# Attention scale turned once and spread through DRAM, part of the memory features moved from GpSimd to VectorE, and other matmul durations in the planner

## The chip, the cores and the metric

The kernel runs on one core of one Trainium2 chip. The metric is the device time of one execution in microseconds (us). The trace comes from one profiled execution of the same kernel. Engine names are those of the profile: PE is TensorE, DVE is VectorE, ACT is ScalarE, POOL is GpSimd, and SP is the sync engine, which issues nearly all transfers.

## The reference

Three stages follow each other: an attention with a recurrent memory, and two feed-forward blocks. B, H, S, D are 4, 8, 576, 64.

```python
def _attn_ref(q, k, v, M_prev, z_prev, beta):
    scores = np.where(causal, -1e9, scale * np.matmul(q, k.transpose(0, 1, 3, 2)))
    a = np.exp(scores - scores.max(-1, keepdims=True))
    a /= a.sum(-1, keepdims=True) + 1e-09
    local = np.matmul(a, v)
    def phi(x):
        return np.where(x > 0, x, np.exp(x) - 1.0) + 1.0
    q_p = phi(q)
    mem_ret = np.einsum('bhsd,bhde->bhse', q_p, M_prev)
    mem_norm = np.einsum('bhsd,bhd->bhs', q_p, z_prev)[..., None] + 1e-06
    g = 1.0 / (1.0 + np.exp(-beta))[None, :, None, None]
    return g * mem_ret / mem_norm + (1 - g) * local

x = attn_out.transpose(0, 2, 1, 3).reshape(B * S, H * D)   # 2304 x 512
h = x @ w_in                                               # 512 -> 2048
x = (np.maximum(h, 0) + np.log1p(np.exp(-np.abs(h)))) @ w_out
out = ((x @ w_a) * (x @ w_b)) @ w_out2                     # 512 -> 1536 -> 512
```

## The kernel before

**Attention in units.** A unit is one batch and one pair of heads; there are 16. The two heads lie on the upper and lower 64 partitions. For a unit the kernel computes five blocks of scores (`score(0)` to `score(4)`, matmuls of L494 and L510), takes each row's minimum on VectorE (L498, L511), the exponential and its row sum on ScalarE (L502, L515), turns the exponentials on TensorE (L558, L575, L576), copies them out with the gate applied (L564 on ScalarE, L566, L578 and L579 on VectorE), and multiplies by V (L588, L612). Everything after the scores of a unit runs one turn of the loop later, between the scores of the next unit.

**The memory path.** `prep_v` and `prep_v2` make the features phi(q) = exp(min(q, 0)) + max(q, 0): GpSimd takes the minimum (L476), ScalarE the exponential (L477) and the relu (L478), GpSimd the sum (L481). `memory` multiplies them by M and z (L525), and VectorE forms 1/(norm * rs) and the scaled product mo (L529 to L531). The product is turned (L600) and accumulated with the attention's in one PSUM bank.

**The scale.** rs is 1 / (sum of the exponentials), a column per row block and head (128 x 10). The finished product lies turned (features on partitions, rows along the free axis), so rs is needed as a row, repeated on 64 partitions. Before, `over` widens rs into R with GpSimd (L547), `spread` turns R with four transposes (L596), ScalarE copies the result out of PSUM (`rb`, L597), and `finish` does the same for the last 64 rows with two small matmuls (L620) and a copy (L624). VectorE then forms xx = product * rb (L608, L625), and xx is stored to `xs` in DRAM (L630).

**The feed-forward stages** use a fast matrix scheme (seven products for eight) with operands split in a high and a low part. `left_parts` decodes a weight block and splits it (rows of L708 to L712, L721, L321, L328), `right_parts` splits the activations (`x1h`, `x1l` and so on), `spill` decodes a block of the next weights and stores it. `BEFORE1` says ahead of which product unit of the first stage these are recorded (`w` a weight block, `x` an activation block, `s` a spill). The products are L826 (first and third stage) and L968.

**What sets the order.** No instruction is issued where the code stands. `Plan` records every step with what it reads and writes, `weigh` gives it a modelled duration, and `order` runs a list scheduler over engines; `emit` writes each engine's queue in the planned order. Attention is stream 0, the feed-forward stages are stream 1; on TensorE stream 0 goes first and inside a stream the code's order holds. On the other engines the step with the longest way to the end goes first. Steps that read and write SBUF only on VectorE or GpSimd carry `port`: the plan keeps VectorE's and GpSimd's apart in time, and a later GpSimd step waits for the VectorE step ahead of it. Each engine then works through its queue in order.

## Time and profile before

| | |
|---|---|
| median of 3 runs | 958.6 us (958.4 to 958.77) |
| profiled execution | 958.62 us, span 956.8 us |
| busy share: PE, DVE, ACT, POOL | 98%, 84%, 61%, 15% |
| TensorE clock granted | 1.00 of full speed over the whole span |
| attention, first product to last | 4.8 to 208.7 us |

The span is the stretch from the first to the last instruction; the execution's own time is 1.8 us longer. A busy PE is counted from records of pipelined matmuls, so the stage is read from the stretches and the waits as well. GpSimd works only in the attention.

### The profile page before, as it was taken

What the parts mean: (1) busy time and instruction counts of PE and PEld (TensorE: products, weight loads), DVE (VectorE), ACT (ScalarE), POOL (GpSimd) and SP (SyncE); (2) the same over time, 40 slices, a digit from 0 to 9 for tenths busy, and PEclk for the clock granted to TensorE, in tenths of its full rate; (3) what the DMA queues carried; (4) which work ended last, traced back from release to release, by engine and by line L of the source; (5) the groups of instructions that cost most, each with busy time, mean ns of one, the idle gap of its engine ahead of it and who ended that gap; (6) DMA issues with size and microseconds to landing.
All of it is one profiled execution on the core that took longest, in us unless ns stands there. A gap on an engine that the chain in (4) does not pass through costs nothing.

```text
span 956.8 us, 17107 instructions
## 1 busy us (share of the span) xinstructions
PE 938.2 (98%) x6316; PEld 898.7 (94%) x6316; DVE 803.7 (84%) x1491; ACT 579.8 (61%) x1156; POOL 139.4 (15%) x149
## 2 busy tenths in 40 slices
PE   6999999999999999999999999999999999999998
PEld 5887777789999999999999999999999999999998
DVE  4898788887999994998769999999999656899683
ACT  6988888876766666664445665444444334464443
POOL 8877767400000000000000000000000000000000
PEclk9999999999999999999999999999999999999999
DMA  7433444216699889746351243556554236762701
GB/s 239 118 111 112 135 131 119 76 59 229 210 318 317 308 297 369 310 150 222 116 198 50 93 140 136 179 199 237 190 184 154 97 114 209 264 204 85 231 34 50
DMA packets 82308, 167.33 MB, mean 175 GB/s; under 512 B 11568, under 2 KB 63536, under 8 KB 76976
## 3 DMA queue, kind: packets, MB, share of 16 engines
q1 hardware_dynamic: 81792, 165.91, 51.8%
q8 instruction: 49, 0.80, 0.3%
q10 hardware_dynamic: 432, 0.33, 0.1%
q14 instruction: 35, 0.29, 0.1%
HBM read 106.18 MB, written 60.03 MB: 174 GB/s over the span
## 4 chain that ended last, share of the span: by engine, by line
PE 90%; ACT 3%; POOL 3%; DVE 2%; DMA 1%; issue 1%; SPq 0%; DVEq 0%; POOLq 0%; ACTq 0%
PE bank L826 45%; PE bank L968 32%; PE bank L588 3%; PE bank L525 2%; PE bank L558 2%; POOL ph L476 2%; PE bank L494 2%; ACT eTrue L502 1%; PE bank L575 1%; ACT ph L477 1%; PE bank L612 1%; PE bank L596 1%; PE bank L600 1%; ACT aT L564 1%; PE bank L510 0%
## 5 line engine op out<-in xcount | busy, mean ns | idle before, releaser
L331 DVE TENSOR_TENSOR s<-bank,s 128x384 f32<-128x384 f32 x216 | 117.7, 554 | 35.5 <-PE bank L826 31.6
L804 ACT ACTIVATE s<-bank 128x384 f32<-128x384 f32 x72 | 34.9, 487 | 78.0 <-PE bank L826 45.3
L328 DVE TENSOR_TENSOR t<-t,t 128x1536 f32<-128x1536 f32 (+1 forms) x48 | 74.6, 1554 | 0.6
L826 PE MATMUL bank<-x1h,w 128*128 128x384 f32 x240 | 70.9, 336 | 1.5 <-ACT w L321 1.1
L826 PE MATMUL bank<-x7h,w 128*128 128x384 f32 x240 | 70.6, 334 | 0.9 <-ACT s L807 0.9
L826 PE MATMUL bank<-x5h,w 128*128 128x384 f32 x240 | 70.6, 334 | 0.0
L826 PE MATMUL bank<-x2h,w 128*128 128x384 f32 x240 | 70.5, 334 | 0.0
L826 PE MATMUL bank<-x3h,w 128*128 128x384 f32 x240 | 70.5, 334 | 0.0
L826 PE MATMUL bank<-x6h,w 128*128 128x384 f32 x240 | 70.5, 334 | 0.0
L826 PE MATMUL bank<-x4h,w 128*128 128x384 f32 x240 | 70.5, 334 | 0.0
L321 ACT ACTIVATE w<-wf 128x256 fp32r<-128x256 f32 (+1 forms) x100 | 50.0, 500 | 17.7 <-DVE w L328 11.1
L328 DVE TENSOR_TENSOR w<-wf,w 128x256 fp32r<-128x256 f32 (+1 forms) x100 | 53.3, 535 | 5.7 <-ACT w L321 5.5
L801 ACT ACTIVATE s<-bank 128x384 f32<-128x384 f32 x72 | 35.0, 487 | 35.3 <-PE bank L826 21.8
L862 ACT ACTIVATE s<-s 128x384 f32<-128x384 f32 x72 | 37.4, 522 | 27.3 <-DVE s L331 27.0
L321 ACT ACTIVATE gx2h<-t 128x768 fp32r<-128x768 f32 x37 | 31.3, 847 | 33.4 <-PE bank L968 30.9
L321 ACT ACTIVATE gx1h<-t 128x768 fp32r<-128x768 f32 x37 | 31.4, 847 | 33.2 <-PE bank L968 33.2
L321 ACT ACTIVATE gx0h<-t 128x768 fp32r<-128x768 f32 x37 | 31.4, 847 | 31.3 <-PE bank L968 28.1
L710 ACT ACTIVATE raw<-raw 128x512 f32<-128x512 f32 (+1 forms) x54 | 42.7, 802 | 10.6 <-DVE raw L709 9.7
L328 DVE TENSOR_TENSOR gx0l<-t,gx0h 128x768 fp32r<-128x768 f32 x37 | 35.4, 957 | 14.6 <-ACT gx0h L321 13.0
L807 ACT ACTIVATE s<-bank 128x384 f32<-128x384 f32 x72 | 35.3, 490 | 19.2 <-PE bank L826 14.6
L328 DVE TENSOR_TENSOR gx1l<-t,gx1h 128x768 fp32r<-128x768 f32 x37 | 35.4, 955 | 13.3 <-ACT gx1h L321 13.0
L321 ACT ACTIVATE gx3h<-t 128x768 fp32r<-128x768 f32 x36 | 30.5, 847 | 26.4 <-PE bank L968 26.4
(327 smaller groups left out, 3120.4 us busy)
## 6 DMA issues: line engine op xcount, KB each, us to landing
gs<-s SPq DMA_DIRECT2D x96, 192.0 KB, 4.5
t<-gs SPq DMA_DIRECT2D x24, 768.0 KB, 5.5
us<-s SPq DMA_DIRECT2D x72, 192.0 KB, 2.6
t<-us SPq DMA_DIRECT2D x12, 768.0 KB, 5.0
raw<-w_in SPq DMA_DIRECT2D x8, 1024.0 KB, 6.2
raw<-w_out SPq DMA_DIRECT2D x8, 1024.0 KB, 6.4
raw<-w_a SPq DMA_DIRECT2D x6, 1024.0 KB, 6.5
raw<-w_b SPq DMA_DIRECT2D x6, 1024.0 KB, 5.2
```

The costliest lines, as they stand in the source:

```text
L321: A.activation(out=o, in_=i, func=AF.Copy)
L328: eng.tensor_tensor(out=o, in0=a, in1=b, op=ALU.subtract)
L331: eng.tensor_tensor(out=o, in0=a, in1=b, op=ALU.add)
L476: G.tensor_scalar(out=self.ph, in0=self.qr, scalar1=0.0, scalar2=0.0, op0=ALU.min, op1=ALU.add)
L588: PE.matmul(out=self.po[both[j], 128 * k :], lhsT=self.vr[:, k, 64 * j : 64 * j + 64], rhs=a, start=False, stop=k == 3, skip_group_check=True,
L710: A.activation(out=f(high), in_=f(high), func=AF.Identity, scale=REBIAS)
L801: A.activation(out=self.s1, in_=bank["b"], func=AF.Copy)
L804: A.activation(out=self.s5, in_=bank["c"], func=AF.Copy)
L807: A.activation(out=self.s2, in_=bank["b"], func=AF.Copy)
L826: PE.matmul(out=o, lhsT=w(n, a, k), rhs=x[n][c][:, k], start=start and k == t == 0, stop=k == 1 and t == 2, skip_group_check=True,)
L862: A.activation(out=s, in_=s if bank is None else bank, func=AF.Softplus)
L968: PE.matmul(out=o, lhsT=self.w[n][a][:, u, 128 * m : 128 * m + 128], rhs=x[c][:, j], start=start and u == t == 0, stop=u == self.nu - 1 an ...
```

## The change

Four edits. First, in 14 of the 16 units (all but the first and the last, `near`) `send` turns rs once (128 x 10 to 10 x 128) right behind the memory products, copies it to SBUF on VectorE, writes it to DRAM (`rsd`, two transfers) and reads it back repeated on 64 partitions (two transfers, one for each head). R, its four transposes, the two small matmuls and both copies of ScalarE are kept for the two `near` units only. `rb` has two buffers. Second, ScalarE takes exp(q) without GpSimd's minimum, and one VectorE instruction forms min(exp(q), 1) + max(q, 0); both GpSimd steps go. Third, the plan takes other durations for plain fp32 products with 64 rows, and counts half a switch between transposes and products of one tiling. Fourth, `BEFORE1` records one spill ahead of product unit 18 in place of 7, and the ring of `s` buffers is listed in another order.

```diff
         if name not in self.state:
             return
+        if name in self.whole:
+            yield None, 1
+            return
...
-                s.mode = 128, 128
+                s.mode = 128, 128, True
...
-                s.time = max(2 * (n / 1.2 + 3) if plain else n / 2.4 + 13.3, cols * 0.42 * (128 // rows))
+                s.time = (1 + plain) * max(n / 1.2 + 3 if plain else n / 2.4 + 13.3, cols * 0.42 * (128 // rows))
...
-                        end += SWITCH
+                        end += SWITCH if not mode or s.mode[:2] != mode[:2] else SWITCH // 2
...
+    rsd = [kept([2, 5, 128], f"rsd{i}") for i in range(B * NP)]
+    plan.whole.update(t.tensor.name for t in rsd)
...
-            G.tensor_scalar(out=self.ph, in0=self.qr, scalar1=0.0, scalar2=0.0, op0=ALU.min, op1=ALU.add)
-            A.activation(out=self.ph, in_=self.ph, func=AF.Exp)
+            A.activation(out=self.ph, in_=self.qr, func=AF.Exp)
             A.activation(out=self.pos, in_=self.qr, func=AF.Relu)
 
         def prep_v2(self):
-            G.tensor_tensor(out=self.ph, in0=self.ph, in1=self.pos, op=ALU.add)
+            V.scalar_tensor_tensor(out=self.ph, in0=self.ph, scalar=1.0, in1=self.pos, op0=ALU.min, op1=ALU.add)
...
+            if not self.near:
+                self.send(banks[0:10, 0, 352:480])
...
+        def send(self, turned):
+
+            rt = take("rt")
+            PE.transpose(out=turned, in_=self.rs, identity=ident)
+            V.tensor_copy(out=rt[0:10], in_=turned)
+            d = rsd[self.b * NP + self.p]
+            SP.dma_start(out=d[:, 0:4].rearrange("j c q -> c j q"), in_=rt[0:8])
+            SP.dma_start(out=d[:, 4, 0:64], in_=rt[8:9])
+            for j, r in enumerate(both):
+                SP.dma_start(out=self.rb[r], in_=d[j].rearrange("c q -> (c q)")[0:S].partition_broadcast(64))
...
+            self.near = self.b * NP + self.p in (0, B * NP - 1)
+            if self.near:
+                self.R = blocks(take("R"))
...
-        0: "w0 w1 x0", 1: "x1", 3: "x2", 5: "w2", 7: "w3 s", 8: "s", 10: "w4 s", 11: "s", 13: "w5 s", 14: "s", 16: "w6 s", 17: "w7 s", 20: "t",
+        0: "w0 w1 x0", 1: "x1", 3: "x2", 5: "w2", 7: "w3", 8: "s", 10: "w4 s", 11: "s", 13: "w5 s", 14: "s", 16: "w6 s", 17: "w7 s",
+        18: "s", 20: "t",
```

On TensorE the order stays row for row, but for the removed and the added rows and six products of the first stage that move inside the last unit. On the other engines it moves throughout. Three places follow; line numbers of the changed kernel are shifted.

**VectorE, behind the memory products of the seventh unit.** nm is 1/(norm * rs), mo the scaled memory product, aT the turned exponentials, eTrue the row minima of the next scores, xx the finished product, rb the spread scale. Before:

```order
L529 SCALAR_TENSOR_TENSOR nm_124<-bank,rs_128 128x2x5
L530 RECIPROCAL nm_124<-nm_124 128x10
L531 TENSOR_TENSOR mo_100<-bank,nm_124 128x2x5x64
L566 TENSOR_SCALAR aT_112<-bank,og_60 128x512
L498 ISA eTrue_83,mn_123<-bank,mask_56 128x384
L498 ISA mn_123 128x1
L498 ISA eTrue_84,mn_123<-bank,mask_56 128x384
L498 ISA mn_123 128x1
L498 ISA eTrue_85,mn_123<-bank,mask_56 128x512
L498 ISA mn_123 128x1
L566 TENSOR_SCALAR aT_114<-bank,og_60 128x512
```

The same place in the changed kernel:

```order
L537 SCALAR_TENSOR_TENSOR nm_127<-bank,rs_131 128x2x5
L548 COPY rt_105<-bank 10x128
L538 RECIPROCAL nm_127<-nm_127 128x10
L539 TENSOR_TENSOR mo_100<-bank,nm_127 128x2x5x64
L589 TENSOR_SCALAR aT_114<-bank,og_60 128x512
L503 ISA eTrue_83,mn_126<-bank,mask_56 128x384
L503 ISA mn_126 128x1
L503 ISA eTrue_84,mn_126<-bank,mask_56 128x384
L503 ISA mn_126 128x1
L632 TENSOR_TENSOR xx_122<-bank,rb_120 128x512
L589 TENSOR_SCALAR aT_116<-bank,og_60 128x512
L650 TENSOR_TENSOR xx_122<-bank,rb_120 128x64
```

The copy of the turned scale stands between nm and its reciprocal, and the two xx rows here are those of the unit before; they stood at the end of their own unit.

**VectorE, the end of the same unit.** eT is the minimum of the fifth block of scores, a the tail's turned exponentials, w and wf are weight preparation, eFalse the first scores of the next unit. Before:

```order
L511 ISA eT_96,mn_123<-bank,mask_57 128x576
L511 ISA mn_123 128x1
L578 TENSOR_TENSOR aT_106<-bank,og_60 128x512
L579 TENSOR_TENSOR a_115<-bank,og_60 128x128
L328 TENSOR_TENSOR w<-wf,w 128x256
L721 TENSOR_TENSOR wf<-wf 128x256
L545 RECIPROCAL rs_129<-ss_127 128x10
L608 TENSOR_TENSOR xx_118<-bank,rb_117 128x512
L625 TENSOR_TENSOR xx_118<-bank,rb_117 128x64
L498 ISA eFalse_87,mn_122<-bank,mask_56 128x128
```

In the changed kernel:

```order
L601 TENSOR_TENSOR aT_108<-bank,og_60 128x512
L602 TENSOR_TENSOR a_117<-bank,og_60 128x128
L516 ISA eT_96,mn_125<-bank,mask_57 128x576
L516 ISA mn_125 128x1
L486 SCALAR_TENSOR_TENSOR ph_76<-ph_76,pos_78 128x640
L331 TENSOR_TENSOR w<-wf,w 128x256
L746 TENSOR_TENSOR wf<-wf 128x256
L503 ISA eFalse_87,mn_125<-bank,mask_56 128x128
```

The new sum of the features (ph) stands behind the last minimum of the unit. Further rows of weight preparation now stand between the next unit's minima and its nm, where before nothing stood.

**VectorE, the seventh weight block of the first feed-forward stage.** raw, wf and w are its decoding and its split, plain and more a spill, s the sums of the products. Before:

```order
L708 TENSOR_SCALAR raw_62<-raw_62 128x512 x2
L709 SCALAR_TENSOR_TENSOR raw_62<-raw_62 128x512 x2
L331 TENSOR_TENSOR s_141<-bank,s_141 128x384
L711 TENSOR_SCALAR raw_62<-raw_62 128x512 x2
L712 SCALAR_TENSOR_TENSOR wf<-raw_62 128x2x256 x2
L721 TENSOR_TENSOR wf<-wf 128x256
L331 TENSOR_TENSOR s_132<-bank,s_132 128x384
L721 TENSOR_TENSOR wf<-wf 128x256
L331 TENSOR_TENSOR s_131<-bank,s_131 128x384
L721 TENSOR_TENSOR wf<-wf 128x256 x2
L328 TENSOR_TENSOR w<-wf,w 128x256 x2
```

In the changed kernel:

```order
L736 TENSOR_SCALAR raw_63<-raw_63 128x512
L737 SCALAR_TENSOR_TENSOR wf<-raw_63 128x2x256 x2
L746 TENSOR_TENSOR wf<-wf 128x256
L737 SCALAR_TENSOR_TENSOR plain_146<-raw_62 128x1024
L334 TENSOR_TENSOR s_139<-bank,s_139 128x384
L746 TENSOR_TENSOR wf<-wf 128x256
L334 TENSOR_TENSOR s_138<-bank,s_138 128x384
L746 TENSOR_TENSOR wf<-wf 128x256 x2
L746 TENSOR_TENSOR more_149<-plain_147,more_149 128x256
L746 TENSOR_TENSOR more_148<-plain_146 128x256
L331 TENSOR_TENSOR w<-wf,w 128x256
```

Ahead of the last row of each piece stand, counted from the start of the stage, 48 sums of products and six decoded spills before, and 42 sums and five decoded spills in the changed kernel.

## Rows read from the trace of the kernel before

**Rows 1.** The page: an engine's busy time, then the chain that ended last.

```profile
PE 938.2 (98%) x6316; PEld 898.7 (94%) x6316; DVE 803.7 (84%) x1491; ACT 579.8 (61%) x1156; POOL 139.4 (15%) x149
...
PE 90%; ACT 3%; POOL 3%; DVE 2%; DMA 1%; issue 1%; SPq 0%; DVEq 0%; POOLq 0%; ACTq 0%
```

**Rows 2.** Stretches: length, busy us of each engine, granted clock, DMA share, GB/s.

```profile
30.70:89.00 58.30, 57.86 (x635) 47.20 (x636) 52.44 (x165) 51.57 (x142) 45.72 (x44) 1.00 0.41 119
89.00:188.10 99.10, 94.73 (x1016) 75.64 (x1016) 84.61 (x251) 86.16 (x236) 66.72 (x64) 1.00 0.39 117
...
255.00:350.00 95.00, 93.82 (x540) 93.18 (x539) 88.26 (x170) 64.58 (x129) 0.00 (x0) 1.00 0.89 303
```

**Rows 3.** Waits of PE over the span: us in total, times, longest.

```profile
PE bank L494 <- DVE kh L323: 5.1, 2, 4.8
PE bank L558 <- ACT aT L564: 3.6, 8, 0.8
PE bank L494 <- POOL kl L328: 1.5, 1, 1.5
PE bank L525 <- POOL mz L438: 1.2, 1, 1.2
PE bank L826 <- ACT w L321: 1.1, 1, 1.1
PE bank L826 <- ACT s L807: 0.9, 1, 0.9
```

**Rows 4.** The chain that ended last, from 138 us on: start, us, what.

```profile
140.19 2.36 POOL ph L476
...
142.57 0.74 ACT ph L477
...
144.43 0.57 ACT aT L564
```

**Rows 5.** PE's instructions in order of time, 48.7 to 53 us: start, us.

```profile
48.74 0.27 PE L576 MATMUL bank<-ident,eT 128*128 128x128 f32 x1
48.85 0.60 PE L596 MATMUL bank<-ident,R 128*128 128x128 f32 x4
49.29 0.60 PE L600 MATMUL bank<-ident,mo 128*128 128x128 f32 x4
...
52.61 0.29 PE L618 MATMUL bank<-ident,mo 128*64 128x64 f32 x4
52.72 0.29 PE L620 MATMUL bank<-ident,rs 128*64 128x64 f32 x4
52.94 0.33 PE L494 MATMUL bank<-kh,qh 64*128 64x128 f32 x2
```

**Rows 6.** Groups by form, 16.2 to 208.7 us: busy us, mean ns, idle before.

```profile
L476 POOL TENSOR_SCALAR ph<-qr 128x640 f32<-128x640 f32 x15 | 35.2, 2350 | 5.2 <-PE bank L525 5.2
...
L531 DVE TENSOR_TENSOR mo<-bank,nm 128x640 f32<-128x640 f32 x16 | 13.2, 825 | 0.5
...
L597 ACT ACTIVATE rb<-bank 128x512 f32<-128x512 f32 x16 | 9.4, 589 | 0.1
...
L579 DVE TENSOR_TENSOR a<-bank,og 128x128 f32<-128x128 f32 x16 | 4.5, 280 | 0.0
...
L712 DVE SCALAR_TENSOR_TENSOR wf<-raw 128x512 uint32<-128x512 uint32 x4 | 2.8, 694 | 0.1
```

**Rows 7.** DVE's and POOL's instructions in order of time, 94.2 to 98.3 us.

```profile
97.42 0.90 DVE L328 TENSOR_TENSOR w<-wf,w 128x256 fp32r<-128x256 f32 x1
...
96.62 1.42 POOL L328 TENSOR_TENSOR kl<-kr,kh 128x576 fp32r<-128x576 f32 x1
```

**Rows 8.** The group of the same DVE instruction, 209 to 360 us.

```profile
L328 DVE TENSOR_TENSOR w<-wf,w 128x256 fp32r<-128x256 f32 x18 | 7.6, 421 | 2.8 <-ACT w L321 2.7
```

**Rows 9.** Waits of DVE, 16.2 to 208.7 us.

```profile
DVE nm L529 <- PE bank L525: 12.6, 16, 2.9
```

**Rows 10.** DMA issues, 16 to 209 us: KB each, median us to landing.

```profile
vr<-vt SPq DMA_DIRECT2D x13, 32.0 KB, 2.7
```

More of the change, by code (lines that the diff above doesn't have):

```diff
@@ L61, in __init__ @@
         self.tc, self.steps, self.state, self.place, self.over = tc, [], {}, {}, {}
-        self.stream, self.exps, self.last = 0, [], {}
+        self.stream, self.exps, self.last, self.whole = 0, [], {}, set()
     def buffer(self, name, words, at, dtype=F32):
@@ L170, in weigh @@
                 rows, cols = (64 if x <= 64 else 128 for x in (kw["lhsT"].partition_size(), size(kw["lhsT"])))
-                s.time = max(2 * (n / 1.2 + 3) if plain else n / 2.4 + 13.3, cols * 0.42 * (128 // rows))
+                s.time = (1 + plain) * max(n / 1.2 + 3 if plain else n / 2.4 + 13.3, cols * 0.42 * (128 // rows))
                 s.time /= 16384 / rows / cols
-                s.mode = rows, cols
+                s.mode = rows, cols, False
         elif s.eng == "DVE":
@@ L390, in tile_kernel @@
     put("mz", NP * 65, spare(NP * 65), spare(NP * 65))
-    put("R", 512, late(512))
+    put("rt", 128, late(128), late(128))
+    put("R", 512, spare(512))
     put("aT", 512, *(late(512) for _ in range(10)))
     put("a4", 128, late(128), late(128))
-    put("rb", S, late(S))
+    put("rb", S, late(S), late(S))
     put("xx", S, late(S), late(S))
@@ L521, in memory @@
             nm = take("nm")
-            s = ps("psS", True)[:, :, 0:325].rearrange("p j (c e) -> p j c e", c=5)
+            banks = ps("psS", True)
+            s = banks[:, :, 0:325].rearrange("p j (c e) -> p j c e", c=5)
             for c in range(5):
@@ L545, in over @@
             V.reciprocal(out=rs, in_=self.ss)
-            self.R = R = blocks(take("R"))
-            G.tensor_scalar(
-                out=R.rearrange("p c (j e) -> p c j e", j=2), in0=heads(rs[:, 0:8], 4), scalar1=1.0, scalar2=0.0, op0=ALU.mult, op1=ALU.add,
-            )
+            self.rb = take("rb")
+            self.near = self.b * NP + self.p in (0, B * NP - 1)
+            if self.near:
+                self.R = blocks(take("R"))
+                G.tensor_scalar(
+                    out=self.R.rearrange("p c (j e) -> p c j e", j=2), in0=heads(rs[:, 0:8], 4), scalar1=1.0, scalar2=0.0,
+                    op0=ALU.mult, op1=ALU.add,
+                )
         def turn(self, eng, cols):
@@ L571, in turn_tail @@
             s = ps("psT")
-            self.a, self.a4, self.rb = a, a4, _ = take("aT"), take("a4"), take("rb")
+            self.a, self.a4 = a, a4 = take("aT"), take("a4")
             self.pt = pt = ps("t")
@@ L593, in spread @@
         def spread(self):
-            pr = ps("psS", True)[:, 0]
-            for c in range(4):
-                PE.transpose(out=pr[:, 128 * c : 128 * c + 128], in_=self.R[:, c], identity=ident)
-            A.activation(out=self.rb[:, 0:512], in_=pr, func=AF.Copy)
+            if self.near:
+                pr = ps("psS", True)[:, 0]
+                for c in range(4):
+                    PE.transpose(out=pr[:, 128 * c : 128 * c + 128], in_=self.R[:, c], identity=ident)
+                A.activation(out=self.rb[:, 0:512], in_=pr, func=AF.Copy)
             self.po = ps("o")
@@ L618, in finish @@
                 PE.matmul(out=pt[r, 0:64], lhsT=mo[:, 4, h], rhs=ident[:, h], start=False, stop=True, skip_group_check=True)
-            for j, r in enumerate(both):
-                PE.matmul(
-                    out=pt[r, 64:128], lhsT=self.rs[:, 8:9].to_broadcast([128, 64]), rhs=ident[:, 64 * j : 64 * j + 64],
-                    start=True, stop=True, skip_group_check=True,
-                )
-            A.activation(out=rb[:, 512:576], in_=pt[:, 64:128], func=AF.Copy)
+            if self.near:
+                for j, r in enumerate(both):
+                    PE.matmul(
+                        out=pt[r, 64:128], lhsT=self.rs[:, 8:9].to_broadcast([128, 64]), rhs=ident[:, 64 * j : 64 * j + 64],
+                        start=True, stop=True, skip_group_check=True,
+                    )
+                A.activation(out=rb[:, 512:576], in_=pt[:, 64:128], func=AF.Copy)
             V.tensor_tensor(out=xx[:, 512:576], in0=pt[:, 0:64], in1=rb[:, 512:576], op=ALU.mult)
@@ L877, in prepare1 @@
         if kind == "t":
-            put("s", HALF, *(47104 + HALF * i for i in range(6)), *(53760 + HALF * i for i in range(5)))
+            put("s", HALF, *(53760 + HALF * i for i in range(5)), *(47104 + HALF * i for i in range(6)))
             return
```

## The prediction

> **What bounds the kernel now.** I read the page first. TensorE is busy for 98% of the span, and the chain that ended last is 90% TensorE [rows 1]. So a change counts only where it takes work from TensorE's queue or a wait ahead of it. The waits of TensorE say which there are [rows 3]: one start-up wait for the first operands (4.8 us, which stays), eight waits of the transposes L558 for ScalarE's copy L564 (3.6 us), two waits for GpSimd at the start (1.5 and 1.2 us), and two in the first feed-forward stage (1.1 and 0.9 us).
>
> Then the stretches, cut at starts of the memory products L525 [rows 2]. From 30.7 to 89.0 us lie five units at 11.66 us each, in which TensorE misses only 0.44 us in all: this is TensorE's own pace. From 89.0 to 188.1 us lie eight units at 12.39 us each, 0.73 us slower, and TensorE's work is the same. Over all 13 units the period is 157.4 / 13 = 12.11 us. The chain says why the later ones are slow [rows 4]: GpSimd's minimum L476 (2.36 us) releases ScalarE's exponential, behind which the exponential of the scores and the copy L564 stand in ScalarE's queue, and L558 waits for that copy. The other number to keep is VectorE: 52.44 + 84.61 = 137.05 us busy in those 13 units, 10.54 us per unit. It idles 1.17 us per unit in the first five. The granted clock is 1.00 throughout (the 2.4 GHz level) and plays no part.
>
> **The change part by part.**
>
> *TensorE's own work, 14 units.* Four transposes L596 take 49.29 - 48.85 = 0.44 us. The two products L620 (four instructions) take 0.11 us: L618, of the same size, starts at 52.61 and L620 at 52.72; another 0.11 us up to L494 is the change of tiling, which stays [rows 5]. Removed: 0.55 us. Added is one transpose with a 128-column moving operand. The nearest row is the single transpose L576, 0.11 us. It stands between L525 and L558, where the tiling changes already, but its ten output rows are a shape that no row shows, so it costs between 0.11 and 0.33 us (two more changes at 0.11); I take 0.15 because it is a transpose of full depth like its neighbour. Net -0.40 us per unit, which makes TensorE's own pace 11.66 - 0.40 = 11.26 us.
>
> *The wait for GpSimd's minimum.* L476 goes, the exponential reads q directly and can run as soon as q has landed, a unit ahead; ScalarE also loses the copy L597 of 589 ns [rows 6] and the small copy L624. So the chain of [rows 4] is cut at its head, and if nothing took its place the eight slow units would fall to TensorE's pace as well.
>
> *What VectorE gets.* One scalar_tensor_tensor over 640 columns per unit. The nearest rows are the same operation over 512 columns, 694 ns, and a tensor_tensor over 640 columns out of PSUM, 825 ns [rows 6]; both overlap their neighbours by some 60 to 80 ns, so I take 0.75 us (bounds 0.69 and 0.87). The copy of rt from PSUM, 128 columns, has L579 as its nearest row, 280 ns with overlap; I take 0.20 us (0.15 to 0.28). VectorE's work per unit becomes 10.54 + 0.95 = 11.49 us, which is more than TensorE's 11.26. This is the term that decides: VectorE becomes the pace. What it idles now is mostly its wait at nm for L525: without the first unit's 2.9 us it is (12.6 - 2.9) / 15 = 0.65 us per unit [rows 9]. In the new order rows of weight preparation stand in that place, so the wait is filled with work. I leave 0.15 us per unit for what stays (an estimate; 0 if VectorE always has work, up to 0.65 if it still waits as before). The period is then 11.64, and I use 11.65 us. Over 13 units: 13 x (11.65 - 12.11) = -6.0 us. It holds only because the later part of the unit has room: behind the sum ph, TensorE still has L600, L588 and L612, so VectorE's delay there meets nobody for some microseconds; the five faster units gain almost nothing.
>
> *The scale's way through DRAM.* Four small transfers per unit on SP's queue. A 32 KB load takes 2.7 us from issue to landing [rows 10]; the write and the read back follow each other, 5.4 us, plus SP's issue of the loads of q, k and the store of the unit before that now stand among them. The consumer, xx, has moved a unit on: it stands behind the next unit's memory products and four minima. From the copy of rt to xx lies a whole period (11.65 us) and the seven rows between, some 14 us, against 6 to 9 us. So I cost it at nothing; cover is about 5 us. If it were late, VectorE would stand at xx, with the minima of the 512-wide scores behind it, which TensorE's next transposes need. rb's second buffer and the rt pair make reuse no issue: they come back two units later.
>
> *Start.* The first unit's two GpSimd steps (L476 alone 2.35 us [rows 6]) stand ahead of the second unit's kh, ql, kl and of mz. Without them TensorE's waits for kl (1.5) and mz (1.2) shrink [rows 3]; ScalarE's q for the second unit bounds the gain. I take -1.5 us (bounds -0.5 and -2.5).
>
> *Last units.* After 188.1 us there is one more unit without the transposes, -0.4 us.
>
> *First feed-forward stage.* TensorE's order is unchanged there. From 255 to 350 us VectorE is busy 88.26 of 95 us [rows 2], and TensorE waits once for a weight block, the seventh, 1.1 us by the list of waits and some 1.5 us with its second half [rows 3]. In the new order this block stands behind 42 sums and five spills where it stood behind 48 and six, so it comes earlier by more than the attention shrinks. I take the wait away, -1.5 us. The other wait (ScalarE, 0.9 us) is left as it is.
>
> *The planner's durations* have no cost of their own; they act by the orders above.
>
> Sum: -6.0 - 0.4 - 1.5 - 1.5 = -9.4 us on the profiled execution's 958.62 us, that is 949.2 us (its time equals the median of 958.6).
>
> **The rivals.**
>
> *TensorE stays the pace.* If VectorE's operations overlap well enough for 11.26 us per unit, the 13 units give 13 x (11.26 - 12.11) = -11.1, and the total is -14.5: 944.1 us. For it: in the first five units VectorE carried 10.49 us in 11.66 without holding TensorE. Against it: 11.49 us of work do not fit into 11.26.
>
> *VectorE keeps half or all of its old gaps.* With 0.65 us in place of 0.15 the period is 12.14, the units gain nothing, and what stays is start, end and weight wait: -3.0, 955.6 us. With part of it, 951 to 957.
>
> *VectorE's new sum stands behind GpSimd (slower).* At 97.42 us VectorE's subtraction of 256 columns took 0.90 us, where 18 of the same take 421 ns; GpSimd's kl ran until 98.04, and VectorE ended 0.28 us later [rows 7, 8]. So an SBUF-only VectorE operation that meets a GpSimd operation is held until that one ends. The new sum ph is of this kind, and kl (1.42 us) and ql run on GpSimd about when it comes up. If it is held for c us in each of 13 units and VectorE is the pace, the total is -9.4 + 13 c: no gain from c = 0.72, over 0.2% slower from 0.87, and 962 us at c = 1.0. For it: the plan keeps the two apart only in planned time. Against it: GpSimd loses L476's 2.35 us and two further steps of its 66.72 / 8 = 8.3 us per unit [rows 2, 6], so fewer meetings remain. The Trainium skill, page "SBUF — State Buffer", section "SBUF: two separate sides", states this as an exclusive lock between GpSimd and a VectorE operation with two SBUF inputs, held for the whole instruction; by that rule the trace agrees.
>
> *The scale comes late.* If the way through DRAM took over 14 us, VectorE would stand at xx in 14 units; 0.75 us late each eats the gain (about 959 us), and more makes it slower. Against it is the cover of 5 us.
>
> **How the numbers follow.** I give the forecast (946.5 to 952.5) 0.50, TensorE as the pace (942.5 to 946.5) 0.20, VectorE with its old gaps (952.5 to 958) 0.18, the held sum 0.08, the late scale 0.04. The range from 943.5 to 956 leaves out some of the second, the end of the third and the last two cases, about 2 in 10. A measurement here tells about 0.2%, 1.9 us. Faster than that is the forecast, TensorE's pace and most of the third case, 0.83; within it 0.08; slower 0.09, nearly all from the held sum and the late scale.
>
> **What would show it.** Right: the starts of L525 stand 11.5 to 11.8 us apart in every unit, VectorE is busy over 95% of the stretch, L558's waits for L564 are gone, and the last product of the attention ends some 8 us earlier. The weight wait near 341 us is gone. Wrong: L525 every 11.2 to 11.3 us (VectorE fits), or every 12 or more with a long ph on VectorE (held), a wait of VectorE at nm near 0.6 us (gaps stay), or one at xx for a transfer (late scale).

## The result and the profile after

The changed kernel takes 946.3 us (median of 4, 945.79 to 947.24) against 958.5 us (4 runs, 958.4 to 958.77). The ratio is 0.9873, with a 95% interval of 0.9856 to 0.989. It is 12.2 us faster, where 9.4 us were forecast.

First the page of the kernel after: busy time by engine, then the chain that ended last by engine. It answers to [rows 1].

```profile
PE 931.2 (99%) x6218; PEld 891.3 (94%) x6218; DVE 815.5 (86%) x1521; ACT 573.9 (61%) x1128; POOL 69.3 (7%) x103
...
PE 89%; DVE 10%; issue 1%; ACT 0%; DMA 0%; POOL 0%; DVEq 0%; ACTq 0%; POOLq 0%
```

TensorE lost 7.0 us of busy time, GpSimd half of its own, and GpSimd and ScalarE are gone from the chain (3% each before). VectorE is now in it with 10%, where it had 2%. That is some 94 us, about half of the attention's time, so by the chain alone VectorE is a candidate for the pace.

Next the waits of TensorE over the span (total, times, longest), which answer to [rows 3].

```profile
PE bank L499 <- DVE kh L326: 4.9, 1, 4.9
PE bank L499 <- POOL kl L331: 1.2, 1, 1.2
PE bank L531 <- POOL mz L444: 1.2, 1, 1.2
PE bank L531 <- DVE mn L503: 0.8, 3, 0.3
PE bank L581 <- ACT aT L587: 0.3, 1, 0.3
...
```

Of the eight waits of the transposes (now L581) for the copy aT one is left, and the two waits of the first feed-forward stage are gone from the list. The first three rows are the start.

Then the stretches: length, and the busy us of TensorE, its weight loads, VectorE, ScalarE and GpSimd. They answer to [rows 2]; the first is the 13 units, from the second memory product (L531) to the fifteenth, the second the seventh weight block's time.

```profile
29.10:177.30 148.20, 147.07 (x1563) 116.29 (x1561) 144.72 (x432) 130.26 (x349) 50.66 (x63) 1.00 0.49 141
...
250.00:345.00 95.00, 95.00 (x550) 95.00 (x549) 86.79 (x169) 63.52 (x128) 0.00 (x0) 1.00 0.91 301
```

The 13 units take 148.2 us, 11.40 us each, against 157.4 us (12.11 each). TensorE misses 1.13 us in all of them, and VectorE is busy 144.72 / 148.20 = 97.7%, 11.13 us per unit. In the second stretch TensorE misses nothing, where the kernel before missed 1.18 us.

Where the time came from, by the starts of the first memory product of each unit and the start of the last matmul (953.03 before, 940.19 after):

| part | forecast | measured |
|---|---|---|
| start of the first memory products (16.25 to 14.83), and the first interval (14.44 to 14.28) | -1.5 | -1.6 |
| 13 units (157.4 to 148.2) | -6.0 | -9.3 |
| the interval after them (10.70 to 10.42) | -0.4 | -0.3 |
| from the last memory products on (754.2 to 752.5), the weight wait in it | -1.5 | -1.7 |
| sum | -9.4 | -12.8 |

The two profiled executions are 12.8 us apart, the medians 12.2. So three of four terms were right within 0.2 us, and the 13 units gave 3.3 us more. In nine of the 13 the starts stand 11.24 to 11.42 us apart, in one 11.48; three are 11.54 to 11.57.

The next rows are from the kernel after in order of time (start, us): GpSimd's ql and VectorE's feature sum ph in one unit, then the sum of the next unit, where ql ran later.

```profile
94.21 1.56 POOL L331 TENSOR_TENSOR ql<-qr,qh 128x640 fp32r<-128x640 f32 x1
...
94.77 1.68 DVE L486 SCALAR_TENSOR_TENSOR ph<-ph,pos 128x640 f32<-128x640 f32 x1
...
106.11 0.82 DVE L486 SCALAR_TENSOR_TENSOR ph<-ph,pos 128x640 f32<-128x640 f32 x1
```

The sum takes 0.82 us alone, and 1.68 us when ql runs at its issue: ql ends at 95.77, and the sum 0.68 us later. In eight units it took 1.68 to 1.71. The Trainium skill (page "SBUF — State Buffer", section "SBUF: two separate sides") states an exclusive lock between GpSimd and a VectorE operation with two SBUF inputs; by that rule the trace agrees. The rival of the held sum did come about, at some 0.6 us per unit over the 0.75 that I took, and the units were still faster than forecast. That left one question open: is VectorE, 97.7% busy, the pace of the units at all?

### The profile page after: what moved, and what is told of

It reads as the page before. It is cut to its first block, busy times and chain, and to the rows that moved or that the text cites. A ratio compares the mean times of both kernels' runs of the same rounds, so it can differ in the third digit from the quotient of the medians.

```text
span 944.0 us, 16943 instructions
## 1 busy us (share of the span) xinstructions
PE 931.2 (99%) x6218; PEld 891.3 (94%) x6218; DVE 815.5 (86%) x1521; ACT 573.9 (61%) x1128; POOL 69.3 (7%) x103
## 4 chain that ended last, share of the span: by engine, by line
PE 89%; DVE 10%; issue 1%; ACT 0%; DMA 0%; POOL 0%; DVEq 0%; ACTq 0%; POOLq 0%
PE bank L851 46%; PE bank L994 32%; PE bank L499 2%; PE bank L611 2%; DVE eTrue L503 2%; PE bank L581 2%; PE bank L531 2%; DVE ph L486 1%; DVE aT L589 1%; DVE mo L539 1%; PE bank L515 1%; DVE eT L516 1%; DVE eFalse L503 1%; DVE aT L601 1%; PE bank L636 0%
## 5 line engine op out<-in xcount | busy, mean ns | idle before, releaser
L324 ACT ACTIVATE w<-wf 128x256 fp32r<-128x256 f32 (+1 forms) x100 | 49.8, 499 | 17.0 <-DVE w L331 12.2
L735 ACT ACTIVATE raw<-raw 128x512 f32<-128x512 f32 (+1 forms) x54 | 42.7, 802 | 12.3 <-DVE raw L734 11.8
L507 ACT ACTIVATE eTrue<-eTrue,mn 128x384 f32<-128x384 f32 (+1 forms) x64 | 42.2, 663 | 9.5 <-DVE mn L503 9.5
```

What stands on the lines that cost most here:

```text
L324: A.activation(out=o, in_=i, func=AF.Copy)
L507: A.activation(out=e, in_=e, func=AF.Exp, scale=-1.0, bias=mn[:, n : n + 1], accum_out=sm[:, n : n + 1])
L735: A.activation(out=f(high), in_=f(high), func=AF.Identity, scale=REBIAS)
```

## The experiments

Two theories stood against each other. **VectorE is the pace**: 11.13 us of work and what it waits make 11.40 us (my forecast's step, with the size off). **TensorE is the pace**: its own 11.25 us and small waits make 11.40, and VectorE is full because the planner puts weight preparation for the next stage into every hole. The kernels fall into two groups: parts of the change alone, and one cost added or taken away. This table has the results; the columns of us are read from the starts of memory products and the last matmul in each trace ("tail": from the last memory products to the last matmul). Each ratio is to runs of the kernel before that were taken along with it (medians of 958.5 to 958.7 us).

| kernel | median us | ratio to before (95%) | first product | each of 13 units | tail |
|---|---|---|---|---|---|
| before | 958.5 | 1 | 16.25 | 12.11 | 754.2 |
| after | 946.3 | 0.9873 (0.9856 to 0.989) | 14.83 | 11.40 | 752.5 |
| features alone | 958.6 | 0.9997 (0.9987 to 1.0006) | 14.78 | 11.67 | 760.8 |
| durations alone | 961.8 | 1.003 (1.0019 to 1.0041) | 16.35 | 12.40 | 752.7 |
| after without features | 961.2 | 1.0028 (1.0017 to 1.0039) | 16.40 | 12.00 | 758.1 |
| after, old durations | 948.1 | 0.9887 (0.9872 to 0.9902) | 15.70 | 11.42 | 754.2 |
| after, old spill order | 947.6 | 0.988 (0.9863 to 0.9896) | 14.70 | 11.40 | 753.3 |
| after, ql behind the sum | 953.0 | 0.9938 (0.9924 to 0.9953) | 15.33 | 11.38 | 759.0 |
| after, one more VectorE row | 954.7 | 0.996 (0.9945 to 0.9975) | 16.89 | 11.60 | 758.4 |
| after, two matmuls fewer | 949.1 | 0.9899 (0.9884 to 0.9914) | 14.83 | 11.25 | 758.0 |
| after, rt on ScalarE | 961.6 | 1.003 (1.002 to 1.004) | 15.50 | 12.05 | 757.5 |
| after, one hop more | 967.6 | 1.0085 (1.0067 to 1.0102) | 15.26 | 12.69 | 758.1 |
| after, two hops more | 997.8 | 1.0404 (1.0387 to 1.0422) | 14.75 | 14.74 | 758.0 |
| after, kh and kl first | 945.6 | 0.9861 (0.9846 to 0.9876) | 15.09 | 11.41 | 752.4 |

### Parts of the change

**Features alone.** The kernel before with this edit only:

```diff
-            G.tensor_scalar(out=self.ph, in0=self.qr, scalar1=0.0, scalar2=0.0, op0=ALU.min, op1=ALU.add)
-            A.activation(out=self.ph, in_=self.ph, func=AF.Exp)
+            A.activation(out=self.ph, in_=self.qr, func=AF.Exp)
...
-            G.tensor_tensor(out=self.ph, in0=self.ph, in1=self.pos, op=ALU.add)
+            V.scalar_tensor_tensor(out=self.ph, in0=self.ph, scalar=1.0, in1=self.pos, op0=ALU.min, op1=ALU.add)
```

> The kernel before with the feature edit alone (exponential straight from q, minimum and sum in one VectorE instruction), without the way through DRAM and with the planner's old durations. If the chain behind GpSimd's minimum is what made the eight later units slow, and TensorE's own pace of 11.66 us stays: 13 x (11.66 - 12.11) = -5.9, start -1.5, so about 951 us, and no wait of the transposes for the copy aT. If the held sum decides (0.5 us more in half the units) and the copies stay on ScalarE, the late units remain slow and only the start is gained: about 957 us. If the chain wasn't the cause at all: 957 us too, with the waits of the transposes still there.

The time is that of before, but the trace shows the expected gain and a loss that eats it. These are its 13 units (columns as above):

```profile
29.21:180.89 151.68, 151.31 (x1653) 123.39 (x1651) 139.00 (x416) 135.69 (x370) 58.54 (x78) 1.00 0.36 113
```

And from its list of TensorE's waits the longest:

```profile
PE bank L825 <- ACT w L321: 5.3, 1, 5.3
```

Twelve of the 13 units are 11.63 to 11.65 us, and TensorE misses 0.37 us in all. So GpSimd's two feature steps were the cause of the slow units (the edit takes both away at once; the chain of [rows 4] names the minimum), and the 11.66 us that I took for the pace without that chain was right. With the start that is -7.2 us up to the fifteenth memory products (188.13 to 180.89). In the first feed-forward stage a weight block comes 5.3 us late and the tail is 6.6 us longer. Part of this is the clock: behind that wait the granted clock is 0.50 in the stretch from 340 to 344 us, and TensorE's products run slower there. The planner had put less of the preparation beside the attention, where VectorE had the sum to do (on the tile raw, of which more below, 17.5 us in place of 22.0); that this made the block late is likely, but no run shows it by itself.

**Durations alone.** The kernel before with the planner's new durations:

```diff
-                s.time = max(2 * (n / 1.2 + 3) if plain else n / 2.4 + 13.3, cols * 0.42 * (128 // rows))
+                s.time = (1 + plain) * max(n / 1.2 + 3 if plain else n / 2.4 + 13.3, cols * 0.42 * (128 // rows))
...
-                        end += SWITCH
+                        end += SWITCH if not mode or s.mode[:2] != mode[:2] else SWITCH // 2
```

> The kernel before with the planner's new durations alone. No instruction is added or taken away, only places in the queues can move. If the durations have no weight of their own: 958.5 +- 1 us. If they are what takes the later units out of the chain behind GpSimd's minimum (rival): 13 units at 11.66 us, about 952 us.

It is 3 us slower, which neither expectation had. The units are 12.40 us and the waits for aT have grown, while the tail is 1.5 us shorter: the weight wait near 341 us is gone by this edit alone. From the list of TensorE's waits:

```profile
PE bank L558 <- ACT aT L564: 6.5, 12, 1.3
```

**After without the features.** The kernel after with minimum and sum back on GpSimd (the first diff turned round).

> The kernel after without the feature edit: minimum and sum of the features back on GpSimd, all else kept (way through DRAM, planner's durations, spill order). If TensorE's own pace is what counts everywhere: 14 units x -0.40, so about 953 us. If the chain behind GpSimd's minimum sets the later units whatever TensorE does: gain only in five units, about 956 us, with the transposes' waits for aT grown. If VectorE is the pace of the kernel after, this one, which has 0.8 us per unit less for it, is as fast as after in its units, and only the start (1.6 us) is lost: 948 us.

Its units are 12.00 us, 0.40 less than with the durations alone, as large as the term for TensorE's own work (-0.55 + 0.15). The chain behind GpSimd still sets these units, as its list of TensorE's waits shows in the first row; the second row is the largest piece of the tail's loss, the rows gx2 at the border of the two feed-forward stages.

```profile
PE bank L582 <- ACT aT L588: 5.9, 12, 1.2
...
PE bank L995 <- ACT gx2h L324: 2.6, 1, 2.6
```

That VectorE has less work here than in the kernel after and the units are 0.6 us longer speaks against its work as the pace, but not alone, since the chain explains it.

**After with the old durations.**

> The kernel after with the planner's old durations; no instruction added or taken away. My reading so far: alone, the new durations made the kernel before slower in its units (12.40 in place of 12.11 us) and took the weight wait near 341 us away. If they only act on that wait: units at 11.40 us as in after, the tail 1.5 us longer or, as in the run with the features alone, 8 us longer (a weight block 5 us late): 948 to 954 us. If the new durations are what lets the units run at TensorE's pace: units at 11.6 us or more, 950 to 957 us. If they do nothing here: 946.3 us.

The units are those of after (11.42): with GpSimd's chain gone the new durations no longer harm them. By the trace they give 0.8 us up to the last memory products and 1.7 us in the tail; the medians differ by 1.8 us, with intervals that overlap. The weight wait near 341 us is not back with the old durations either.

**After with the old spill order** and the old list of what is prepared when:

```diff
-            put("s", HALF, *(53760 + HALF * i for i in range(5)), *(47104 + HALF * i for i in range(6)))
+            put("s", HALF, *(47104 + HALF * i for i in range(6)), *(53760 + HALF * i for i in range(5)))
```

> The kernel after with the old order of the spill ring and the old list of what is prepared when in the first feed-forward stage. If the weight wait near 341 us went because of the new order of these: it is back, and the time is 1.5 us over after, 947.8 us. If it went because the attention's order left fewer sums ahead of the block (my step): same as after, 946.3 +- 0.5 us.

The intervals of this kernel and of after overlap, so the medians' difference of 1.3 us isn't shown. The trace has no weight wait near 341 us. The other gap, from one product's start to the next, which was 1.23 us near 382 us before and 0.44 after, is 1.23 us here, and the tail is 0.8 us longer. So the spill order and its list are worth that gap, and the weight wait went by the planner's order. The count of sums and spills that I gave as its reason isn't needed, since the durations alone removed it with the old lists.

### VectorE or TensorE

**ql behind the sum.** The kernel after, with GpSimd's ql made to wait until VectorE's sum has run, so that the two don't meet:

```diff
                 sub(e, self.ql[:, q], qr[:, q], f(self.qh[:, q]))
+                if e is G and plan.summed:
+                    plan.steps[-1].deps.add(plan.summed)
...
             V.scalar_tensor_tensor(out=self.ph, in0=self.ph, scalar=1.0, in1=self.pos, op0=ALU.min, op1=ALU.add)
+            plan.summed = len(plan.steps) - 1
...
-            if nxt and n:
-                nxt.prep_k()
             if cur:
                 cur.prep_v2()
+            if nxt and n:
+                nxt.prep_k()
```

> The kernel after with GpSimd's ql put behind VectorE's feature sum, so that the two no longer meet (in half the units of after the sum was held by ql, 1.70 us in place of 0.82). If VectorE is the pace: it gets back 0.86 us in half the units, the units fall to TensorE's own 11.25 us, 13 x -0.15 = -1.9, so 944.4 us. If TensorE is the pace: 946.3 +- 0.5 us with VectorE's sum at 0.82 us in all units. If ql, now later, holds other VectorE instructions in its turn: no change, with the longer means elsewhere.

The group of the sum in the 13 units (busy us, mean ns), first of the kernel after, then of this one:

```profile
L486 DVE SCALAR_TENSOR_TENSOR ph<-ph,pos 128x640 f32<-128x640 f32 x13 | 17.7, 1364 | 0.0
```

```profile
L488 DVE SCALAR_TENSOR_TENSOR ph<-ph,pos 128x640 f32<-128x640 f32 x13 | 10.7, 826 | 0.0
```

This kernel's 13 units as a stretch, and then VectorE's longest wait in them:

```profile
29.54:177.50 147.96, 147.20 (x1560) 116.27 (x1560) 141.30 (x434) 129.52 (x350) 51.86 (x64) 1.00 0.48 143
```

```profile
DVE nm L540 <- PE bank L550: 4.4, 6, 0.9
```

The hold is gone: 0.83 us in place of 1.36, 7.0 us in 13 units. The period stays: 11.38 us in place of 11.40. VectorE took part of the time for more weight preparation and waited for TensorE (nm) with the rest; it is 95.5% busy. It has also left most of the chain that ended last, as the page of this kernel shows:

```profile
PE 92%; DVE 4%; issue 0%; DMA 0%; ACT 0%
```

So the held sum had no price, because VectorE's total was not the pace, though in the kernel after half of the attention's chain ran through it. The whole kernel is slower by its tail (+6.5 us), where gx2 comes late as in the kernel without features, and by 0.5 us at the start.

**One more VectorE row.** The kernel after with one instruction more per unit:

```diff
+            V.scalar_tensor_tensor(out=self.ph, in0=self.ph, scalar=1.0, in1=self.ph, op0=ALU.min, op1=ALU.min)
             V.scalar_tensor_tensor(out=self.ph, in0=self.ph, scalar=1.0, in1=self.pos, op0=ALU.min, op1=ALU.add)
```

> The kernel after with one more VectorE instruction of 640 columns per unit, which changes no value (minimum of the feature sum's input with itself and 1, which the sum takes anyway). If VectorE is the pace: its 0.82 us, or 1.3 us with holds by GpSimd, are added to 11.13 us per unit, and the period becomes 12.0 to 12.4: 13 x 0.6 to 1.0 = +8 to +13 us, about 956 us. If TensorE is the pace and VectorE has only work that can lie elsewhere (weight preparation that the planner fills in): the preparation is pushed out of the units and the time stays at 946 to 948 us.

The two groups in its 13 units:

```profile
L486 DVE SCALAR_TENSOR_TENSOR ph<-ph 128x640 f32<-128x640 f32 x13 | 19.3, 1483 | 0.0
L487 DVE SCALAR_TENSOR_TENSOR ph<-ph,pos 128x640 f32<-128x640 f32 x13 | 10.7, 826 | 1.0
```

The 13 units as a stretch, and then TensorE's longest wait in them:

```profile
31.24:182.05 150.81, 147.02 (x1563) 116.29 (x1561) 147.62 (x426) 125.11 (x339) 56.99 (x65) 1.00 0.45 134
```

```profile
PE bank L532 <- DVE mn L504: 2.9, 9, 0.4
```

The two take 30.0 us where after had 17.7, 0.95 us more per unit (the hold by ql now falls on the first). The period grew by 0.20. The rest came out of the preparation. These are the instructions on the tile raw alone in the 13 units, first of after, then of this kernel; behind the length stands VectorE's busy us, then ScalarE's.

```profile
29.10:177.30 148.20, 19.32 (x31) 10.28 (x19) 1.00 0.49 141
```

```profile
31.24:182.05 150.81, 13.88 (x23) 7.82 (x15) 1.00 0.45 134
```

By the groups of VectorE that write raw, wf, w and the rows x, preparation in the 13 units sums to 30.6 us before, 25.2 after and 15.3 here. Outside the units the kernel loses 2.1 us up to the first memory products and 5.9 us in the tail. Of these, 4.4 us come early in the first feed-forward stage with a weight block that is 1.9 us late, behind which the granted clock is 0.50 from 246 to 248 us. That the block is late because its preparation was put off is likely, but no run shows it by itself. My second expectation had the right mechanism and no price for the tail.

**Two matmuls fewer.** The kernel after without the kh and ql products of the fifth score block (that block loses precision):

```diff
-                for t, (a, b) in enumerate(terms):
-                    PE.matmul(out=s[:, c, :288], lhsT=a[:, 512:640], rhs=b[:, cs], start=t == 0, stop=t == 2)
+                for t, (a, b) in enumerate(terms[:2]):
+                    PE.matmul(out=s[:, c, :288], lhsT=a[:, 512:640], rhs=b[:, cs], start=t == 0, stop=t == 1)
```

> The kernel after without the product of kh with ql in the fifth block of scores: two matmuls of 288 columns per unit (0.13 us each) are left out, so that block's scores have less precision; TensorE's other rows stay in their order, and VectorE has as much work as before. If TensorE is the pace in the units of after: 0.26 us less per unit, 11.14 us, 13 x -0.26 = -3.4 and a little at both ends, 942.5 us. If VectorE is the pace: 11.40 us per unit as in after, 946 us. Since VectorE was busy 11.13 us per unit, a mixture (11.2 to 11.3 us) would say that both are near their limit.

Its 13 units:

```profile
28.92:175.19 146.27, 145.49 (x1537) 112.54 (x1535) 142.21 (x434) 130.33 (x349) 49.53 (x64) 1.00 0.46 143
```

The period fell by 0.15 us to 11.25, and six units are at 11.13 to 11.14. TensorE's removed work is 0.26 us. From the start of that block to the last transposes behind it (L515 to L599) the time falls by 0.10 us only, so 0.16 us per unit is lost again to waits right there. VectorE is busy 10.94 us per unit, no longer 11.13, with the same instructions of the unit's own: the sum met ql for a shorter time (15.4 us in the 13 units in place of 17.7). This run alone could therefore be read for VectorE as well; the run with ql behind the sum, which took three times as much from the sum and left the period, speaks against it. Taken together, the units follow TensorE by more than half when its work is cut, and don't follow VectorE when its time is cut. The kernel as a whole is 2.8 us slower than after, by a tail that is 5.5 us longer with gx2 late.

**rt on ScalarE.** The kernel after with the copy of the turned scale moved:

```diff
-            V.tensor_copy(out=rt[0:10], in_=turned)
+            A.activation(out=rt[0:10], in_=turned, func=AF.Copy)
```

> The kernel after with the copy of the turned scale moved from VectorE (0.27 us per unit) to ScalarE. If VectorE is the pace of the kernel after (my step, 11.40 us per unit with VectorE 97.6% busy), its units get shorter, at most to TensorE's own pace of 11.25: up to 13 x -0.15 = -1.9, so 944.4 us. If TensorE is the pace and what lies over 11.25 are waits of another origin: 946.3 +- 0.5 us. If ScalarE's copies aT come late by it: up to +2 us, with the transposes' wait for aT back.

It is slower by 15 us, which no expectation had. From its list of TensorE's waits:

```profile
PE bank L499 <- DVE mo L539: 6.4, 9, 1.0
```

And from one unit VectorE and TensorE in order of time (start, us):

```profile
68.30 0.75 DVE L589 TENSOR_SCALAR aT<-bank,og 128x512 f32<-128x512 f32 x1
68.96 0.81 DVE L539 TENSOR_TENSOR mo<-bank,nm 128x640 f32<-128x640 f32 x1
...
69.92 0.50 PE L499 MATMUL bank<-kh,qh 64*128 64x512 f32 x2 [0.95 <-DVE mo L539]
```

In the new plan VectorE takes aT ahead of mo in such units. mo empties the PSUM banks of the memory products, into which the 512-wide scores go next, and TensorE stands 0.95 us. In the 13 units such waits are 5.5 of the 8.5 us that these lose against after; another 5.0 us are the tail, again with gx2 late. VectorE has less to do than in the kernel after; one place in its order costs more than the work saved.

### The scale's way through DRAM, and the start

One and two further copies from DRAM to DRAM on the way, in the kernel after:

```diff
+            for far in hops:
+                o = far[self.b * NP + self.p]
+                SP.dma_start(out=o.rearrange("j c q -> j (c q)")[:, 0:S], in_=d.rearrange("j c q -> j (c q)")[:, 0:S])
+                d = o
```

> The kernel after with two more copies from DRAM to DRAM on the scale's way (each another write and read of the same few KB, by SP's queue), nothing else changed. My step costs this way at nothing under a cover of about 5 us. In the trace of after the read is issued about 5 us before the product xx, and lands some 2.5 us before it. Two hops add about 5 us: if the cover is as forecast, VectorE stands at xx for some 0 to 0.5 us per unit, 946 to 953 us. If the cover is only the 2.5 us, each unit is 2 to 3 us longer, 970 to 985 us. If the planner moves xx a unit further, nothing: 946.3 us.

> The kernel after with one further copy from DRAM to DRAM on the scale's way (two were 3.3 us more per unit). One hop is a transfer of about 2.7 us and its issue on the queue. With a cover of 5 us, as forecast: 946.3 +- 1 us. With the 2.5 us that the trace of after shows between the landing of the scale and the product xx: 0.5 to 1 us more per unit, 953 to 960 us. If it isn't the latency but the further rows on the queue that delay the loads of q, k and v: half of the two hops' price, 1.7 us per unit, 968 us.

One hop costs 1.29 us per unit, two 3.34. Not all of it is waiting: for the same instructions TensorE is busy 153.67 us in the 13 units with one hop and 162.57 with two, where it is 147.07 in after, and the mean granted clock of these stretches is 0.98 and 0.93, where it is 1.00. From the lists of TensorE's waits, one hop, then two:

```profile
PE bank L604 <- DVE xx L655: 10.2, 7, 1.8
```

```profile
PE bank L604 <- DVE xx L655: 30.4, 12, 4.4
```

It isn't VectorE that stands at xx for the scale, as I had it (0.3 us in all with two hops, none with one). xx comes later in VectorE's order, and TensorE stands at the last transpose of the block's tail (L604 here, L599 in after), whose bank xx has to empty. In after xx ends at 115.54 us and that transpose starts at 115.59. So the scale's way is hidden as it is, but there is no room to put xx later. Since the planner moved xx by its own durations for the copies, the runs don't show how late the scale itself would have been, nor what part the queue's further rows have in the price.

**kh and kl first.** The kernel after with the second unit's ql on GpSimd put behind its kl:

> The kernel after with GpSimd's order at the start turned: the second unit's kh and kl ahead of its ql (in after TensorE waits 0.3 us for kh, 1.2 for kl and 1.2 for mz there). If these waits are what is left of the start chain and TensorE is the pace of all that follows: the first memory products stand 0.8 to 1.3 us earlier and the whole kernel gains as much, 945.2 us. If the chain through mz and the held feature sum sets the start in any case: 946.3 us. If the changed row count moves the later plan to the worse order at the boundary of the feed-forward stages: 951 to 953 us with the units unchanged.

No gain: the waits moved. GpSimd's and VectorE's kl in order of time (start, us), and TensorE's wait:

```profile
5.94 1.56 POOL L331 TENSOR_TENSOR kl<-kr,kh 128x576 fp32r<-128x576 f32 x1
...
6.16 2.03 DVE L331 TENSOR_TENSOR kl<-kr,kh 128x256 fp32r<-128x256 f32 x2
```

```profile
PE bank L502 <- DVE kl L331: 2.0, 1, 2.0
```

The first unit's kl on VectorE (0.42 and 0.49 us in after) is held by GpSimd's kl until 7.50 us. TensorE loses at the first unit what it gains at the second. Its 945.6 us can't be told from after, and no kernel here is clearly better than after.

## Why the prediction was right, and where its size was off

**Direction and range** were right: 946.3 us lies in 943.5 to 956. But it lies just outside the forecast's own part of it (946.5 to 952.5) and just inside that of the rival in which TensorE stays the pace (942.5 to 946.5), and the period of 11.40 us lies between the sign of being right (11.5 to 11.8) and that of being wrong (11.2 to 11.3). The step that was to decide the time failed, so the number was met in part by luck.

**The start, the last unit and the weight wait** came out within 0.2 us. The start is the feature edit's (14.78 with it alone, 16.40 without it). The weight wait did go, but my reason for it isn't needed: the planner's durations alone remove it. The agreement of the whole tail (-1.7 us for -1.5) is partly chance: the weight wait gave -1.6 us, the gap near 382 us, which I had left as it is, gave -0.9, and the last unit's end lost 0.8.

**TensorE's own work.** The shortest units are 11.63 us with the features alone and 11.24 in after, -0.39 where -0.40 was forecast; two errors cancel in this. The transposed scale is a row of its own in the order of time of the kernel after:

```profile
40.68 1.54 PE L531 MATMUL bank<-mz,ph 64*128 64x65 f32 x20
42.15 0.28 PE L547 MATMUL bank<-ident,rs 128*10 128x128 f32 x1
42.26 0.38 PE L581 MATMUL bank<-ident,eFalse 128*128 128x128 f32 x2
```

From its start to that of L581 it takes 0.11 us, the low bound of my range, and the transposes behind it take 0.05 us less than they did, so the work fell by 0.50 us. The other 0.10 us are a wait that the lists of waits do not show. Here are VectorE and TensorE in one unit of the kernel after, then TensorE in one of the kernel before (start, us):

```profile
99.25 0.27 DVE L548 COPY rt<-bank 10x128 f32<-10x128 f32 x1
...
99.68 0.82 DVE L539 TENSOR_TENSOR mo<-bank,nm 128x640 f32<-128x640 f32 x1
...
100.56 0.49 PE L499 MATMUL bank<-kh,qh 64*128 64x512 f32 x2
100.89 0.40 PE L499 MATMUL bank<-kl,qh 64*128 64x512 f32 x2
```

```profile
57.00 0.39 PE L494 MATMUL bank<-kh,qh 64*128 64x512 f32 x2
57.23 0.40 PE L494 MATMUL bank<-kl,qh 64*128 64x512 f32 x2
```

In all 13 units of after the first 512-wide scores start 0.05 to 0.06 us behind the end of mo and the next ones 0.33 us behind them; before, the starts stood 0.26 us behind mo and 0.23 apart. With the copy rt ahead of its reciprocal, mo starts 2.29 to 2.47 us behind the memory products, where it was 2.03 with the features alone. The twelve score products L499 between the transposes take 1.55 us on average, where they took 1.42 with the features alone. So TensorE stands some 0.1 us at mo in every unit, and its own pace lies nearer to 11.15 than to the 11.24 of the shortest units (forecast 11.26). That the copy rt is the reason is read from the order of time; the run that moved it to ScalarE changed the order in other ways too.

**The step that failed** is "VectorE's work per unit becomes 10.54 + 0.95 = 11.49 us, which is more than TensorE's 11.26. This is the term that decides: VectorE becomes the pace." Both added prices were too low (the sum 1.36 us with its holds, the copy 0.27), and the step was wrong all the same: the 10.54 us held some 2.35 us of preparation for the next stage (30.6 us / 13), which isn't due in its unit. After the change 25.2 us of it stand there, 0.41 us less per unit, and the tail did not pay for it. What remains between 11.24 and 11.40 is mostly one place: from the last L499 of a unit to its first L531 the starts are 0.355 us apart on average over the 13 units and 0.259 at the least, waiting for VectorE's minimum mn. So TensorE is the pace, with about 0.25 us of short waits for two VectorE rows, mn and mo: it is the place of these rows that counts, not VectorE's sum. The rival that I gave 0.20 had the mechanism; its argument against ("11.49 us of work do not fit into 11.26") is the failed step again.

**GpSimd's feature steps as the cause of the slow units** are shown (features alone: 11.64 us in most units); that it was the minimum rests on the chain. **The held sum** is real, and free here. **The scale's way** cost nothing, as forecast, but the cover may be smaller than the 5 us that I gave. In after xx stands 14.0 to 15.5 us behind the copy rt, as forecast, while the second read is issued only 5.3 to 8.4 us ahead of xx. With the 2.7 us of a load [rows 10] the cover is some 2.6 to 5.7 us (an estimate; no row shows the read's landing).

**What stays open.** Why some plans lose 5 to 6 us with gx2 at the border of the feed-forward stages (six kernels with tails of 757.5 to 759.0 us against 752.4 to 754.2) wasn't tried. TensorE waits some 3.5 us there; the rest is slower products, as the granted clock behind the wait shows (with two matmuls fewer it is 0.50 from 380 to 382 us). The loss comes with changes that have nothing to do with that stage, and it is as large as the effects under study.

## What to carry to other kernels

An engine that is nearly 98% busy, and through which half of the chain runs, need not be the pace if part of its rows can wait: take the movable rows out of its sum first, or cut its work a little and see whether the period follows. Compare single edits by stage and not by the total, since a planner that fills holes can give a gain of 7 us back in a later stage, as the features alone did. Ahead of a wait for a bank the order of two rows counts for more than the work saved, as the copy on ScalarE showed, and a wait of 0.1 us in every unit needn't have a line in the list of waits: the starts of the rows show it.

## What the runs showed of the hardware

- VectorE's 640-column sum of two SBUF tiles took 0.82 us alone and 1.68 to 1.71 when GpSimd's ql ran at its issue. Two subtractions of 0.42 and 0.49 us took 2.03 together behind GpSimd's kl.
- Behind a transpose with ten output rows the next transposes start 0.11 us later.
- At the start TensorE runs at the lower of its two levels for a time. The 20 instructions of the first memory products take 2.47 us in after, and 1.54 us in later units. This is the stretch of the kernel after from 12 to 24 us, with the granted clock third from the end:

```profile
12.00:24.00 12.00, 10.02 (x73) 8.91 (x74) 8.93 (x25) 9.90 (x28) 7.51 (x12) 0.72 0.88 296
```

From 16 to 20 us it is 0.50, the level of 1.2 GHz, and from 22 us on 1.00. In the kernel before the record says 1.00 throughout while its first memory products also take 2.47 us, so "1.00 throughout" in my prediction was read from a record that misses the start. Both kernels begin at that level, and no run separates what it has to do with the gain at the start.

- The granted clock also fell behind long waits of TensorE, and the products behind them ran slower: behind 5.3 us at a weight block (features alone) and behind 2.6 and 1.0 us at gx2 (two matmuls fewer) it was 0.50 for a stretch. Behind the wait of 1.1 us near 342 us in the kernel before it stayed at 1.00.
